# Choosing 256 tokens each of experts 0 and 1 during the last attention unit, and running their matmuls in the gaps of selection

## The chip, the cores and the metric

The kernel runs on one core of one Trainium2 chip. The metric is device time in microseconds (us); lower is better. Several executions are timed. Most of one kernel agree within about 1%; the kernel before has also slower ones (282 to 286 us, mean granted TensorE clock 0.94 to 0.956, against 277 to 280 us at 0.976 to 0.992). An execution over 1.5% above the fastest of its kernel is called slow, and only fast ones are compared here.

## The reference, cut to what matters

```python
x = attention(q, k, v)               # 4 batches x 768 tokens, 8 heads of 64: x is 3072 x 512
logits = x @ w_gate                  # 3072 x 8
order = argsort(-logits.flatten())   # greedy: best (token, expert) pairs first
for idx in order:                    # a token goes to its best expert that has room,
    tok, e = idx // 8, idx % 8       # each expert takes exactly 384 tokens
    if assigned[tok] < 0 and counts[e] < 384:
        assigned[tok] = e; counts[e] += 1
for e in range(8):
    out[assigned == e] = relu(x[assigned == e] @ w1[e]) @ w2[e]   # 512 -> 1024 -> 512
```

No expert knows all its tokens until the whole assignment is known. A few tokens can be known sooner: a token of the first three batches whose logit is high enough for its expert stays there whatever the fourth batch brings.

## The kernel before

Four stages follow one another: attention (eight units; each ends with sums that give its part of the logits), selection (four "rounds", a chain of small VectorE, TensorE and ScalarE steps), dispatch (the chosen tokens become row numbers, the "ids"), and experts. A round, with its useless matmuls that keep TensorE busy:

```python
pk = ps_d.tile([128, 2, 128], FP32, tag="pk")     # a PSUM tile of its own
# ... matmuls into pk ...
pn = ps_d.tile([128, 1], FP32, tag="pn")          # another PSUM tile
# ... matmuls into pn ...
fill(2)                                           # useless matmuls
nc.scalar.activation(Xe[:, nk : nk + 1], pn, AF.Identity, scale=-1.0, bias=bias232)
nc.vector.max(out=mx8, in_=pk)                    # reads pk, while ScalarE reads pn
# ... Xe, ranks; fill(1); next round ...
```

Experts. Each takes three slabs of 128 rows. The rows come by gathers (indirect transfers, one per slab), and the weights of experts 2 to 7 by twelve transfers of 1 MB ("tiles", two per expert). GpSimd issues all of them, and the scatters of the results too, in program order. Four tiles are issued before selection starts; the others here:

```python
gather(0); load_x(0); gather(1)                   # three slabs each
for e in range(8):
    late_weights()                                # one weight tile
    if e + 2 < 8: gather(e + 2)
    late_weights()                                # another
    # up: 32 matmuls of 384 columns, ReLU on ScalarE
    if e + 1 < 8: load_x(e + 1)                   # transposes of the next rows
    # down: 24 matmuls of 512 columns; scatter of each slab
```

`load_x(e + 1)` stands between up and down of expert e. If its rows are not there, the down matmuls wait behind it (6.0 us in the result below).

The softmax here doesn't subtract the row's maximum and nothing guards it: scores larger than these inputs give would overflow.

Of the kernel before, what the change touches and what calls it, by code (L numbers as in the profile page):

```python
# [38 lines left out]
W_EARLY = 2  # L39


@with_exitstack
def kernel(
# [75 lines left out]
    idn = consts.tile([128, NCHUNK], FP32)  # L119

# [8 lines left out]
    @later  # L129
    def _():  # L130
        nc.gpsimd.memset(negones, -1.0)
        nc.gpsimd.memset(bias232, float((32 * 128 - CAP) // 16))

# [40 lines left out]
    @later  # L174
    def _():
        nc.gpsimd.memset(eofs_bf, -63.5)
        iota(eofs_bf[0:1, :, :], [[0, NCHUNK], [CAP, N_EXP]])

# [7 lines left out]
    @later  # L186
    def _():
        for g_ in range(4):
            iota(idn[32 * g_ : 32 * g_ + 32, :], [[S_, B_], [32, NBLK]], base=192 * g_ - N_TOK // 2, cm=1)
        nc.gpsimd.tensor_copy(out=idc[:, ROT:NCHUNK], in_=idn[:, 0 : NCHUNK - ROT])  # L190
        nc.gpsimd.tensor_copy(out=idc[:, 0:ROT], in_=idn[:, NCHUNK - ROT : NCHUNK])

    @later
    def _():
        nc.gpsimd.memset(nb[:, 0:64], 1.0)
        nc.gpsimd.memset(Ub[:, 0:8, :], 0.0)
        nc.gpsimd.memset(Lb[:, 0:8, :], 0.0)

# [24 lines left out]
    QB = 384  # L223

    pctx = ExitStack()
    tp = pctx.enter_context(tc.tile_pool(name="tp", bufs=6, side="right"))
# [3 lines left out]
    with ExitStack() as actx:  # L230
# [4 lines left out]
        rawp = actx.enter_context(tc.tile_pool(name="rawp", bufs=1, side="right"))  # L235
        ttp = actx.enter_context(tc.tile_pool(name="ttp", bufs=4, side="right"))
# [249 lines left out]

        def warm(n):
            for _ in range(n):
                pw = ps_t.tile([128, 512], FP32, tag="pt", name="pw")
                nc.tensor.matmul(pw, lhsT=ones_bf, rhs=ones_bf[:, 0:1].to_broadcast([128, 512]), start=True, stop=True)  # L490
# [6 lines left out]
        if True:  # L497
# [98 lines left out]
            for u in range(2, NU + 1):  # L596
# [57 lines left out]
                for _ in range(3):  # L654
                    if late:
                        late.pop(0)()
                if wpieces:
                    weight_pieces(1 if u < 6 else 2, Bp)
            while late:
                late.pop(0)()  # L660

    w2pool = ctx.enter_context(tc.tile_pool(name="w2pool", bufs=1, reuse_waits="tile"))
    w1_late = [w2pool.tile([128, NKC, F_DIM], BF16, name=f"w1_{e}") for e in range(W_EARLY, N_EXP)]
    w2_late = [w2pool.tile([128, NFC, DM], BF16, name=f"w2_{e}") for e in range(W_EARLY, N_EXP)]
    lates = []
    for e in range(W_EARLY, N_EXP):
        lates.append((w1_late[e - W_EARLY], moe_w1[e].rearrange("(kc p) f -> p kc f", p=128)))
        lates.append((w2_late[e - W_EARLY], moe_w2[e].rearrange("(fc p) d -> p fc d", p=128)))
# [11 lines left out]
    def w1_of(e):  # L680
        return w1_early[:, e, :, :] if e < W_EARLY else w1_late[e - W_EARLY]

    def w2_of(e):
        return w2_early[:, e, :, :] if e < W_EARLY else w2_late[e - W_EARLY]

    idi = consts.tile([128, NCHUNK], I32)
    fi = consts.tile([1, 1], I32)

    def routing(general):
      with ExitStack() as dctx:  # L690
# [28 lines left out]
        def fill(n):  # L719
            for _ in range(n):  # L720
                pw = ps_d.tile([128, 512], FP32, tag="fill", name="pw")
                nc.tensor.matmul(pw, lhsT=ident_bf, rhs=w1_early[:, 0, 0, 0:512], start=True, stop=True)  # L722
# [19 lines left out]
        def fast_round(k, X, Dg):  # L742
            nk = 16 * k
            UB = best(X, Dg)
            pk = ps_d.tile([128, 2, 128], FP32, tag="pk", name="pk")
            for hf in range(2):
# [3 lines left out]
                                    in0=UB[:, 8:32, :], in1=bc_e(mn), op=ALU.is_gt)  # L750
            for hf in range(2):
                nc.tensor.matmul(pk[:, hf, :], lhsT=nb[:, 128 * hf : 128 * hf + 128], rhs=neg_bf,
                                 start=False, stop=True, skip_group_check=True)
            pn = ps_d.tile([128, 1], FP32, tag="pn", name="pn")
            for hf in range(2):
                nc.tensor.matmul(pn, lhsT=nb[:, 128 * hf : 128 * hf + 128], rhs=ones_bf[:, 0:1],
                                 start=(hf == 0), stop=(hf == 1))
            if X is None:
                tok_begin()
            fill(2)  # L760
            Xe = ditp.tile([128, 129], FP32, tag="Xe", name="Xe")
            nc.scalar.activation(Xe[:, nk : nk + 1], pn, AF.Identity, scale=-1.0, bias=bias232)
            mx8 = ditp.tile([128, 8], FP32, tag="mx8", name="mx8")
            nc.vector.max(out=mx8, in_=pk.rearrange("p a b -> p (a b)"))
# [8 lines left out]
            pr2 = ps_d.tile([128, 129], FP32, tag="pr2", name="pr2")  # L773
            nc.tensor.matmul(pr2[:, 0:nk], lhsT=Gm, rhs=Xe[:, 0:nk], start=True, stop=True)
# [4 lines left out]
            rk = ps_d.tile([128, 128], FP32, tag="rk", name="rk")  # L779
            for k0 in range(0, k, 4):  # L780
# [5 lines left out]
                for kk in range(k0, k0 + 4):  # L786
                    nc.tensor.matmul(rk[:, 0:nk], lhsT=Gm_bf, rhs=tg[:, kk, 0:nk],
                                     start=(kk == 0), stop=(kk == k - 1))
            tok_begin()
            fill(1)  # L790
# [22 lines left out]
        def dispatch():  # L813
            pR = ps_d.tile([128, CE], FP32, tag="X", name="pR")
            pc = ps_d.tile([96, 2], FP32, tag="pn", name="pc")
# [4 lines left out]
            nc.tensor.matmul(pR, lhsT=ones_bf[0:2, :], rhs=eofs_bf.rearrange("p c e -> p (c e)"),  # L820
# [10 lines left out]
            MAGIC = 1.5 * 2.0 ** 23  # L831
            hm = ditp.tile([128, NCHUNK], FP32, tag="hm", name="hm")
            nc.vector.tensor_scalar(out=hm, in0=dest, scalar1=1.0 / 128.0, scalar2=MAGIC, op0=ALU.mult, op1=ALU.add)
            hi = ditp.tile([128, NCHUNK], FP16, tag="hi", name="hi")
            nc.vector.tensor_scalar(out=hi, in0=hm, scalar1=-MAGIC, scalar2=None, op0=ALU.add)
            lo = ditp.tile([128, NCHUNK], FP16, tag="lo", name="lo")
            nc.vector.scalar_tensor_tensor(out=lo, in0=hi, scalar=-128.0, in1=dest, op0=ALU.mult, op1=ALU.add)
            fill(9)
# [7 lines left out]
            pI = ps_d.tile([128, NCHUNK], FP32, tag="rk", name="pI")  # L846
# [8 lines left out]
            fill(12)  # L855
# [4 lines left out]
        def general_path():  # L860
# [54 lines left out]
            def count(dst, m):  # L915
                pc = ps_d.tile([128, CE], FP32, tag="X", name="pc")
# [16 lines left out]
            with tc.For_i(0, N_EXP):  # L933
# [21 lines left out]
                pg = ps_d.tile([128, CE], FP32, tag="pk", name="pg")  # L955
# [18 lines left out]
        if True:  # L974
            X, Dg = None, None
# [3 lines left out]
            fill(2)  # L979
            nc.vector.tensor_tensor(out=M, in0=Ub[:, 8:32, :], in1=bc_e(mn), op=ALU.is_le)  # L980
            dispatch()
            pf = ps_d.tile([1, CE], FP32, tag="pr2", name="pf")
            nc.tensor.matmul(pf, lhsT=ones_bf[:, 0:1], rhs=Mf, start=True, stop=True)
            fc8 = dap.tile([1, N_EXP], FP32)
            nc.vector.tensor_reduce(out=fc8, in_=pf.rearrange("p (c e) -> p e c", e=N_EXP), axis=AX.X, op=ALU.add)
            fm = dap.tile([1, 1], FP32)
            nc.vector.tensor_reduce(out=fm, in_=fc8, axis=AX.X, op=ALU.max)
            nc.vector.tensor_single_scalar(out=fi, in_=fm, scalar=capf, op=ALU.is_gt)

    def experts(first):  # L990
        with ExitStack() as fctx:
# [3 lines left out]
            scatters = []  # L995
            xT_of = {}
            xes = {}

            def gather(e):
                for t in range(TSLAB):  # L1000
                    s = TSLAB * e + t
                    xe = gp.tile([128, DM], BF16, tag="xe", name=f"xe_{s}")
                    tc.keep_in_program_order(nc.gpsimd.indirect_dma_start(  # L1003
                        out=xe, out_offset=None, in_=x_tok[:, :],
                        in_offset=bass.IndirectOffsetOnAxis(ap=idi[:, s : s + 1], axis=0),
                    ))
                    xes[s] = xe

            def load_x(e):
                xT_e = fp.tile([128, NKC, TSLAB, 128], BF16, tag="xT_e", name=f"xT_{e}")  # L1010
                for t in range(TSLAB):
# [4 lines left out]
                    nc.vector.tensor_copy(out=xT_e[:, :, t, :], in_=pxe)  # L1016
                xT_of[e] = xT_e

            gather(0)
            load_x(0)  # L1020
            gather(1)
            for e in range(N_EXP):
                xT_e = xT_of.pop(e)
                if first:
                    late_weights()
                if e + 2 < N_EXP:
                    gather(e + 2)
# [3 lines left out]
                for fc in range(NFC):  # L1031
                    ph = ps_h.tile([128, CAP], FP32, tag="ph")
                    for kc in range(NKC):
                        nc.tensor.matmul(ph, lhsT=w1_of(e)[:, kc, 128 * fc : 128 * fc + 128],  # L1034
                                         rhs=xT_e[:, kc, :, :].rearrange("p t n -> p (t n)"),
                                         start=(kc == 0), stop=(kc == NKC - 1))
                    nc.scalar.activation(hT[:, fc, :], ph, AF.Relu)  # L1037
                if e + 1 < N_EXP:
                    load_x(e + 1)
                for t in range(TSLAB):  # L1040
                    po = ps_o.tile([128, DM], FP32, tag="po")
                    for fc in range(NFC):
                        nc.tensor.matmul(po, lhsT=hT[:, fc, 128 * t : 128 * t + 128],  # L1043
# [3 lines left out]
                    s = nc.gpsimd.indirect_dma_start(  # L1047
                        out=out[:, :],
                        out_offset=bass.IndirectOffsetOnAxis(ap=idi[:, TSLAB * e + t : TSLAB * e + t + 1], axis=0),
                        in_=ot, in_offset=None,  # L1050
                    )
                    for prev in scatters:
                        tc.declare_no_dep(s.ins, prev.ins, reason="each token has one expert: the rows written differ")
                    scatters.append(s)
# [4 lines left out]
    gp = ctx.enter_context(tc.tile_pool(name="gp", bufs=9, side="right", reuse_waits="tile"))  # L1059
    fp = ctx.enter_context(tc.tile_pool(name="fp", bufs=2, side="right", reuse_waits="tile"))  # L1060
    hp = ctx.enter_context(tc.tile_pool(name="hp", bufs=2, side="right", reuse_waits="tile"))
    op = ctx.enter_context(tc.tile_pool(name="op", bufs=4, side="right", reuse_waits="tile"))
    experts(True)
    flag = nc.values_load(fi[0:1, 0:1], engines=mybir.ALL_ENGINES)  # L1064
# [38 lines left out]
```

## Time and profile before

282.65 us median of 3 runs (277.18, 282.65 and 496.86; the last is an outlier, and 282.65 is a slow run by the rule above, so the fast state is at 277); the profiled run took 277.43. Stages, read from the starts and ends of the matmuls in the trace:

| event, us from the start | before |
|---|---|
| last attention unit starts | 116.4 |
| its last sums end | 139.4 |
| first selection matmul | 141.3 |
| dispatch starts | 163.9 |
| ids ready | 170.0 |
| first expert matmul | 177.3 |
| expert 2 starts | 199.2 |
| TensorE's last matmul ends | 266.1 |

The same stages as windows (start and end; length; busy time of the matmuls, weight loads, VectorE, ScalarE and GpSimd, with counts; granted clock; DMA share, which counts packets by their start and so can pass 1; GB/s), last unit to the end of TensorE's work:

```profile
116.40:139.40 23.00, 23.00 (x481) 19.67 (x480) 12.14 (x22) 8.73 (x14) 5.37 (x9) 1.00 0.61 109
139.40:141.30 1.90, 0.07 (x3) 0.06 (x1) 1.43 (x6) 0.00 (x0) 1.12 (x2) 1.00 1.05 167
141.30:163.90 22.60, 18.62 (x122) 11.22 (x122) 18.51 (x67) 1.95 (x8) 0.00 (x0) 1.00 1.12 196
163.90:170.00 6.10, 5.57 (x41) 2.65 (x42) 4.46 (x14) 0.00 (x0) 0.00 (x0) 1.00 0.24 49
170.00:177.30 7.30, 5.33 (x28) 1.96 (x27) 1.82 (x6) 0.00 (x0) 5.51 (x6) 1.00 0.29 80
177.30:199.20 21.90, 21.77 (x134) 12.11 (x134) 5.82 (x11) 7.84 (x16) 14.26 (x16) 1.00 1.02 203
199.20:266.10 66.90, 65.81 (x391) 36.05 (x395) 18.24 (x33) 23.52 (x48) 33.01 (x35) 1.00 0.73 185
```

Attention and the experts (rows 1, 6, 7) keep TensorE busy nearly all the time. In selection (row 3) its 18.6 us include useless matmuls.

GpSimd's issues in expert 2 (start, length, engine, line, operation, destination<-source, count, and in brackets the idle time before and what ended it):

```profile
201.38 0.82 POOL L673 DMA_DIRECT2D w<-in_moe_w_dram  x1
202.50 1.00 POOL L1003 DMA_INDIRECT xe<-x_tok,idi  x1 [0.30 <-issue]
...
207.20 0.94 POOL L673 DMA_DIRECT2D w<-in_moe_w_dram  x1 [1.20 <-DMA w<-in_moe_w_dram]
...
214.48 0.81 POOL L673 DMA_DIRECT2D w<-in_moe_w_dram  x1 [2.04 <-DMA w<-in_moe_w_dram]
215.60 0.99 POOL L1003 DMA_INDIRECT xe<-x_tok,idi  x1 [0.31 <-issue]
```

A gather (xe) is issued behind a weight tile (w), and GpSimd sometimes waits until an earlier tile has landed (1.20 and 2.04 us here). With experts of 11.1 us this just keeps up.

### The profile page before, as it was taken

What the parts mean: (1) busy time and instruction counts of PE and PEld (TensorE: products, weight loads), DVE (VectorE), ACT (ScalarE), POOL (GpSimd) and SP (SyncE); (2) the same over time, 40 slices, a digit from 0 to 9 for tenths busy, and PEclk for the clock granted to TensorE, in tenths of its full rate; (3) what the DMA queues carried; (4) which work ended last, traced back from release to release, by engine and by line L of the source; (5) the groups of instructions that cost most, each with busy time, mean ns of one, the idle gap of its engine ahead of it and who ended that gap; (6) DMA issues with size and microseconds to landing.
All of it is one profiled execution on the core that took longest, in us unless ns stands there. A gap on an engine that the chain in (4) does not pass through costs nothing. (4 is left out here: it accounts for less than half of the span.)

```text
span 275.6 us, 7465 instructions
## 1 busy us (share of the span) xinstructions
PE 250.6 (91%) x3174; PEld 172.7 (63%) x3182; DVE 160.0 (58%) x311; ACT 136.3 (49%) x224; POOL 82.6 (30%) x131
## 2 busy tenths in 40 slices
PE   7699899999999999999967878799999999999960
PEld 2577688888888888888844533355565545555520
DVE  3978998888969787774468875322423213233130
ACT  5998969596895959736200000144152250532500
POOL 5040000030508030110330002757665555741240
PEclk9999999999999999999999999999999999999996
DMA  7993889499799978282699990399999999430221
GB/s 275 330 266 66 218 196 275 86 222 261 121 318 160 251 148 182 66 152 62 103 195 206 194 181 13 108 183 187 267 258 263 263 245 290 165 133 10 107 89 36
DMA packets 52568, 49.27 MB, mean 179 GB/s; under 512 B 29744, under 2 KB 44080, under 8 KB 52528
## 3 DMA queue, kind: packets, MB, share of 16 engines
q0 software_dynamic: 15680, 26.22, 45.8%
q1 hardware_dynamic: 36848, 22.50, 31.3%
q8 instruction: 27, 0.44, 0.7%
q14 instruction: 13, 0.11, 0.1%
HBM read 56.05 MB, written 9.44 MB: 238 GB/s over the span
## 5 line engine op out<-in xcount | busy, mean ns | idle before, releaser
L1037 ACT ACTIVATE hT<-ph 128x384 bf16<-128x384 f32 x64 | 31.4, 490 | 69.3 <-PE ph L1034 68.6
L357 ACT ACTIVATE P<-ps 128x860 f32<-128x860 f32 (+1 forms) x46 | 39.4, 895 | 23.2 <-PE ps L339 22.5
L339 PE MATMUL ps<-qT,kA 32*128 32x215 f32 (+2 forms) x864 | 43.6, 333 | 2.5 <-ACT qT L304 2.5
L339 PEld LDWEIGHTS ps<-qT,kA 32*128 32x128 f32 x864 | 37.1, 185 | 7.2 <-ACT qT L304 3.0
L392 PE MATMUL po<-P,v 128*64 128x215 f32 (+6 forms) x576 | 40.6, 292 | 0.2 <-DVE P L372 0.2
L392 PEld LDWEIGHTS po<-P,v 128*64 128x64 f32 x576 | 34.4, 136 | 8.3 <-issue 3.1
L372 DVE TENSOR_TENSOR P<-P,Wm 128x860 f32<-128x860 f32 (+1 forms) x32 | 33.1, 1051 | 9.2 <-ACT P L357 6.5
L1003 POOL DMA_INDIRECT xe<-x_tok,idi x24 | 23.2, 968 | 37.9 <-PE pw L722 29.8
L1046 DVE COPY ot<-po 128x512 f32<-128x512 f32 x24 | 16.4, 691 | 30.2 <-PE po L1043 24.2
L1047 POOL DMA_INDIRECT out_dram<-ot,idi x24 | 23.6, 985 | 30.0 <-DVE ot L1046 27.0
L1034 PE MATMUL ph<-xT,w 128*128 128x384 bf16 x192 | 32.2, 326 | 0.0
L1043 PE MATMUL po<-w,hT 128*128 128x512 bf16 x138 | 31.7, 379 | 0.1
L1043 PEld LDWEIGHTS <-hT 128*128 128x128 bf16 x192 | 18.3, 98 | 19.5
L1016 DVE COPY xT<-pxe 128x512 bf16<-128x512 bf16 x24 | 9.5, 422 | 35.2 <-PE pxe L1015 34.2
L423 PE MATMUL pr<-P,onesx 128*32 128x168 f32 (+11 forms) x768 | 27.6, 259 | 0.0
L1034 PEld LDWEIGHTS <-w 128*128 128x128 bf16 x192 | 18.8, 98 | 13.1
L423 PEld LDWEIGHTS pr<-P,onesx 128*32 128x32 f32 x768 | 24.7, 109 | 2.3 <-issue 0.3
L289 ACT COPY kA<-tT_k 128x720 f32<-128x720 f32 (+2 forms) x18 | 24.4, 1358 | 0.2
L365 DVE TENSOR_TENSOR P<-P,Wm 128x860 f32<-128x860 f32 x16 | 16.3, 1050 | 8.8 <-ACT P L357 8.8
L397 ACT COPY oT<-po 128x384 f32<-128x384 f32 x32 | 14.9, 494 | 8.2 <-PE po L392 8.2
L468 PE MATMUL pk<-ident,oT 128*128 128x128 f32 x96 | 16.5, 288 | 2.2 <-DVE LT L439 2.0
L304 ACT COPY qT<-tT_q 128x768 f32<-128x768 f32 (+1 forms) x11 | 16.5, 1499 | 0.2 <-DVE tT_q L279 0.2
(151 smaller groups left out, 273.0 us busy)
## 6 DMA issues: line engine op xcount, KB each, us to landing
w<-in_moe_w_dram POOLq DMA_DIRECT2D x12, 1024.0 KB, 12.7
v<-in_v_dram SPq DMA_DIRECT2D x32, 180.0 KB, 2.8
kr<-in_k_dram SPq DMA_DIRECT2D x7, 768.0 KB, 4.5
qr<-in_q_dram SPq DMA_DIRECT2D x7, 768.0 KB, 7.6
w_early<-in_moe_w_dram POOLq DMA_DIRECT2D x8, 512.0 KB, 6.6
x_tok<-x SPq DMA_DIRECT2D x32, 96.0 KB, 3.2
w_early<-in_k_dram SPq DMA_DIRECT2D x1, 768.0 KB
w_early<-in_q_dram SPq DMA_DIRECT2D x1, 768.0 KB
```

The source lines that it names most:

```text
L289: nc.scalar.copy(out=kA[:, i0:i1, 8:128].rearrange("p i (c j) -> p i c j", j=NJ), in_=t[:, i0 * NC5 : i1 * NC5, :].rearrange("p (i c) j -> ...
L304: copy(out=qTs[u][:, g, NJ * c0 : NJ * c1].rearrange("p (c j) -> p c j", j=NJ), in_=tTs[f"q{u}", g].rearrange("p j c -> p c j")[:, c0:c1, :])
L339: nc.tensor.matmul(heads[a][:, o : o + w], lhsT=kA[r, gd, i, :], rhs=qTt[r, gd, KT * i : KT * i + w], start=(gd == 0), stop=(gd == 1), ski ...
L357: nc.scalar.activation(P[:, :, 0 : GW[g]], ps[w_][:, :, 0 : GW[g]], AF.Exp, scale=0.125)
L372: tt(out=P[:, :, 0 : GW[g]], in0=P[:, :, 0 : GW[g]], in1=Wm[:, h0 : h0 + 2, lo : lo + GW[g]], op=ALU.mult)
L392: nc.tensor.matmul(po[n][bk][64 * t : 64 * t + 64, a - QB * bk : z - QB * bk], lhsT=v7[:, t, i, :], rhs=P[:, t, o + a - q0 : o + z - q0], ...
L423: nc.tensor.matmul(o_, lhsT=l_, rhs=r_, start=first[gq], stop=True, skip_group_check=True)
L1003: tc.keep_in_program_order(nc.gpsimd.indirect_dma_start(out=xe, out_offset=None, in_=x_tok[:, :], in_offset=bass.IndirectOffsetOnAxis(ap=i ...
L1034: nc.tensor.matmul(ph, lhsT=w1_of(e)[:, kc, 128 * fc : 128 * fc + 128], rhs=xT_e[:, kc, :, :].rearrange("p t n -> p (t n)"), start=(kc == ...
L1037: nc.scalar.activation(hT[:, fc, :], ph, AF.Relu)
L1043: nc.tensor.matmul(po, lhsT=hT[:, fc, 128 * t : 128 * t + 128], rhs=w2_of(e)[:, fc, :], start=(fc == 0), stop=(fc == NFC - 1))
L1047: s = nc.gpsimd.indirect_dma_start(out=out[:, :], out_offset=bass.IndirectOffsetOnAxis(ap=idi[:, TSLAB * e + t : TSLAB * e + t + 1], axis= ...
```

## The change

In the last attention unit the kernel now chooses 256 tokens for each of experts 0 and 1, out of the first three batches, that are certain to stay there, gathers their rows, and lets their transposes and matmuls replace the useless ones in selection and dispatch. The last stage then has one slab for experts 0 and 1 instead of three. To make room for it in PSUM, some tiles of a round were put together. The diff, cut to its core:

```diff
+            e1_min(); ...; e1_pe(); ...; e8_pe()     # early choosing, between the steps of the last unit
+            e8_ids()                                  # early ids; four gathers, one per early slab
 ... cut ...
+        items = [] if general else early_work(ps_d)   # 4 row transposes, 64 up and 32 down matmuls
+        def work(us):                                 # takes items until their cost is used up,
+            ...                                       # useless matmuls when there are none left
 ... cut: in a round ...
-            pk = ps_d.tile([128, 2, 128], FP32, tag="pk", name="pk")
+            pkn = ps_d.tile([128, 512], FP32, tag="pk", name="pkn")
+            pk = pkn[:, 0:256].rearrange("p (a b) -> p a b", a=2)
+            if X is not None:
+                work(0.34)
-            pn = ps_d.tile([128, 1], FP32, tag="pn", name="pn")
+            pn = pkn[:, 256:257]
-            fill(2)
+            work(0.85 if X is not None else 0.6)
-            fill(1)
+            work(0.7)
 ... cut: in dispatch and behind it ...
-            fill(9)
+            work(3.2)
-            fill(12)
+            gather(0, range(ET, TSLAB), False)        # ET = 2: one slab is left
+            gather(1, range(ET, TSLAB), False)
+            gather(2, range(TSLAB), False)
+            while items:
+                work(0.1)
 ... cut: experts ...
+            def slabs(e):
+                return range(ET if first and e < 2 else 0, TSLAB)
                 if first:
                     late_weights()
-                if e + 2 < N_EXP:
-                    gather(e + 2)
+                if e + 2 < N_EXP and not (first and e == 0):
+                    gather(e + 2, slabs(e + 2))
                 if first:
                     late_weights()
```

## The prediction

> **What bounds it now.** TensorE, except in selection (busy time by stretches). Attention's last sums end near 139.4 us. Selection and dispatch (141.2 to 170) are a chain of small VectorE, TensorE and ScalarE steps, 5.2 us a round, whose TensorE gaps hold useless fills. From the first gather (170.3) to the first expert matmul (177.3) are 7 us, also filled. Then 88.8 us of experts, TensorE busy 87.6: 11.1 us each (5.2 up, 0.75 transposes, 5.2 down). Tail 9.5 us.
>
> **Removed (estimates from these durations).** In the last stage experts 0 and 1 have one slab of 128 tokens instead of three. Down loses 32 matmuls of about 0.215 us (6.9 us); up shrinks from 5.2 to about 2 us, twice (6 us); 16 transposes go (1 us): about 14 of 88.8 us. The first expert waits for one gather instead of three: 2.3 us more.
>
> **Added ahead of the experts.**
> - Early selection inside the last attention unit: TensorE 3.4 us (eight rank matmuls 0.5, eighteen id matmuls of 53 ns 0.95, fp32 steps the rest), VectorE 8.5 us, mostly in its idle time. Attention ends about 4.3 us later.
> - Transposes of early rows stand ahead of selection in TensorE's order, their gathers behind two weight pieces: 0.5 to 1.5 us.
> - Early items overrun the fills they replace slightly, and ReLU delays small ScalarE copies: 0.5 to 1 us.
> - In dispatch the down matmuls share one PSUM tile, so each group of eight waits for a ScalarE copy (0.7 to 0.9 us, from 0.49 us for 384 columns); the id matmuls come 1.3 us late.
> Ids come about 7 us later (5.5 to 8.5).
>
> **Where the expert gain goes.** GpSimd's DMA queue works in order: gathers issued at 202.5 and 215.6 landed at 214.6 and 227.4, each 0.4 us after the weight tile issued before them. A weight tile occupies it for 5 us alone, 6 to 7 us among gathers and scatters (landings of consecutive tiles). [...] The changed program issues three weight tiles (two of expert 4, one of 5) just ahead of expert 3's gathers, because experts 0 and 1 now take only 4 us each. I put the first tile 9.4 us after the ids; those gathers then land 28 to 31 us after the ids, while TensorE wants the rows in the middle of expert 2, 19 us after: a stall of 9 to 12 us (down of expert 2 stands behind it in program order), and 0 to 3 us more at experts 4 and 5. From ids to TensorE's end: 96.1 us before, 90 to 95 after.
>
> **Sum.** +7 - 3.5: 277.4 becomes about 280.5 us in the fast state. Without the stall about 270.
>
> **What shows it.** Ids at 177 instead of 170; first remaining expert 5 us after them; TensorE idle some 10 us in the middle of expert 2, released by the DMA into xe, weight tiles landing just before; GpSimd's weight issues waiting on earlier DMAs; experts 6 and 7 back to back at 11 us.
>
> **What would make it wrong.** Gathers overtaking weights, or weight tiles landing in under 5 us: 268 to 272. Early gathers landing late, or more PSUM waits in selection: 284 to 288.
>
> Chances: faster 0.17, within 2% 0.55, slower 0.28. Range 270.5 to 286.5.

## More of the kernel before

From the page of the kernel before: busy tenths in 40 slices of the span, the granted TensorE clock in tenths, and the busy share of the DMA engines.

```profile
PE   7699899999999999999967878799999999999960
PEclk9999999999999999999999999999999999999996
DMA  7993889499799978282699990399999999430221
```

TensorE (PE) is the busy engine, and its granted clock is 1.00 up to the end of its work at 266.1 us.

## The result

The changed kernel takes 288.08 us median (287.06 to 288.64, 4 runs); the kernel before, in the same job, 280.26 (277.18 to 496.86, 4 runs). The ratio is 1.0376, 95% interval 1.0322 to 1.0431: slower. A ratio here is the mean time of one kernel's fast runs over that of the other's, so it is not quite the ratio of the medians; the fast runs of the kernel before were two (277.18 and 277.88), so the loss is 10.4 us. The outputs are correct. The time lies above the range that was predicted.

From the page of the changed kernel, the same three rows:

```profile
PE   7799899999999999899969888848919999999960
PEclk9999999999999999999977999997986999999995
DMA  7992979399996994460589993249999999630221
```

There are two dips: in slices 21 and 22 (the clock is at half from 147.4 to 154.3 us), and in slices 27 to 31 (186 to 222 us), where TensorE is partly idle (busy 25.4 of 36.0 us) and the clock is at half again, from 195.2 to 198.6 and from 212.3 to 219.1 us. In the kernel before neither is there (clock 1.00 up to 271.0 us).

The same stages as windows:

```profile
116.70:146.60 29.90, 27.73 (x526) 23.04 (x525) 18.92 (x53) 9.42 (x16) 7.50 (x12) 1.00 0.51 98
146.60:149.30 2.70, 1.09 (x9) 0.77 (x8) 1.29 (x5) 1.07 (x2) 2.70 (x5) 0.65 0.58 87
149.30:175.80 26.50, 24.17 (x182) 18.64 (x182) 18.85 (x68) 7.61 (x18) 0.91 (x2) 0.91 1.03 178
175.80:183.20 7.40, 6.03 (x49) 3.37 (x50) 4.50 (x15) 1.17 (x2) 2.16 (x3) 1.00 0.30 81
183.20:188.90 5.70, 3.83 (x24) 1.61 (x23) 1.67 (x10) 1.17 (x2) 3.85 (x4) 1.00 0.34 104
188.90:202.30 13.40, 10.04 (x95) 6.81 (x93) 2.30 (x5) 3.95 (x16) 7.91 (x11) 0.87 0.81 158
202.30:277.00 74.70, 68.69 (x397) 37.09 (x395) 18.30 (x33) 23.59 (x48) 35.41 (x37) 0.95 0.78 185
```

Row by row against before: the unit is 6.9 us longer (29.9 against 23.0), the rows' transposes 0.8, the rounds 3.9 with the clock at 0.91, dispatch 1.3. With the unit's start 0.3 later, the ids come at 183.2 and not 170.0, which is 13.2 later. From there to the end of TensorE's work it is 93.8 us (277.0 - 183.2) against 96.1. Experts 0 and 1 are 8.5 us shorter (row 6), and the last row, which is the same work as before, 7.8 us longer.

TensorE in the timeline, lines with idle time before them (start, length, line, operation, operands, count, and in brackets the idle time and what ended it; "issue" means that the profile shows nothing that it waited for):

```profile
144.64 0.32 PE L468 MATMUL pr<-P,onesx 128*32 128x48 f32 x6 [0.26 <-issue]
145.37 0.53 PE L471 MATMUL pr<-oT,wgx 128*32 128x192 f32 x5 [0.41 <-issue]
...
147.51 0.91 PE L989 MATMUL px<-ident_bf,xeE 128*128 128x128 bf16 x7 [0.73 <-issue]
...
191.32 0.38 PE L1395 MATMUL ph<-xT,w_early 128*128 128x128 bf16 x4 [1.27 <-ACT hT L1398]
...
213.68 1.03 PE L1373 MATMUL pxe<-ident_bf,xe 128*128 128x128 bf16 x8 [6.01 <-DMA xe<-x_tok,idi]
```

The same transposes in the kernel before, with no wait ahead of them:

```profile
204.43 0.61 PE L1015 MATMUL pxe<-ident_bf,xe 128*128 128x128 bf16 x8
```

The last line of the changed kernel is the predicted stall: in the middle of expert 2 TensorE waits 6.0 us for the rows of expert 3. The first lines were not predicted: TensorE pauses at the end of attention, and the profile shows nothing that it waits for. I call this starvation below. The line at 191.32 is of the same kind, one engine on: in expert 0 the ReLUs on ScalarE come one in about 1.44 us though their inputs are ready, and TensorE waits for them.

What GpSimd issues around the stall:

```profile
192.60 1.78 POOL L941 DMA_DIRECT2D w<-in_moe_w_dram  x2
...
199.69 0.78 POOL L941 DMA_DIRECT2D w<-in_moe_w_dram  x1
200.78 1.03 POOL L964 DMA_INDIRECT xe<-x_tok,idi  x1 [0.30 <-issue]
202.11 0.99 POOL L964 DMA_INDIRECT xe<-x_tok,idi  x1 [0.30 <-issue]
203.41 0.94 POOL L964 DMA_INDIRECT xe<-x_tok,idi  x1 [0.30 <-issue]
```

Three tiles are issued between the ids and the gathers of expert 3 (200.78 on), and those rows are there at 213.7, 30.5 us after the ids.

One more pair of lines, the maximum on VectorE in a middle round. In the timeline of the kernel before:

```profile
148.61 0.43 DVE L764 MAX8 mx<-pk 128x8 f32<-128x256 f32 x1 [0.38 <-PE pn L756]
```

In that of the changed kernel:

```profile
158.45 0.43 DVE L1113 MAX8 mx<-pkn 128x8 f32<-128x256 f32 x1 [0.83 <-ACT Xe L1110]
```

In the kernel before, the maximum was released by TensorE, after 0.38 us of idle time; now it is released by ScalarE, which reads the neighbouring column of the same PSUM tile, after 0.83 us. Nothing in the arithmetic asks for that, and what puts the maximum behind ScalarE is not in the trace; what is there is 0.45 us more idle time.

### The profile page after: what moved, and what is told of

Its sections match the earlier page's. It is cut to its first block, busy times and chain, and to the rows that moved or that the text cites. A ratio compares the mean times of both kernels' runs of the same rounds, so it can differ in the third digit from the quotient of the medians.

```text
span 286.3 us, 7694 instructions
## 1 busy us (share of the span) xinstructions
PE 251.6 (88%) x3256; PEld 180.3 (63%) x3256; DVE 164.1 (57%) x342; ACT 142.2 (50%) x242; POOL 88.2 (31%) x151
## 5 line engine op out<-in xcount | busy, mean ns | idle before, releaser
L1398 ACT ACTIVATE hT<-ph 128x384 bf16<-128x384 f32 (+1 forms) x64 | 27.5, 438 | 57.1 <-PE ph L1395 53.6
L1404 PE MATMUL po<-w,hT 128*128 128x512 bf16 x144 | 35.0, 396 | 0.0
L1407 DVE COPY ot<-po 128x512 f32<-128x512 f32 x20 | 13.8, 691 | 32.7 <-PE po L1404 30.7
L1374 DVE COPY xT<-pxe 128x512 bf16<-128x512 bf16 x20 | 8.0, 423 | 38.3 <-PE pxe L1373 35.4
L972 POOL DMA_INDIRECT out_dram<-ot,idi x20 | 19.8, 992 | 31.0 <-DVE ot L1407 28.1
L1404 PEld LDWEIGHTS <-hT 128*128 128x128 bf16 x160 | 15.9, 103 | 17.5 <-issue 3.1
L964 POOL DMA_INDIRECT xe<-x_tok,idi x20 | 19.4, 969 | 12.8 <-DMA xe<-x_tok,idi 6.1
L442 ACT COPY oT<-po 128x384 f32<-128x384 f32 x32 | 14.8, 492 | 10.9 <-PE po L437 10.3
```

The source lines that it names most:

```text
L964: ins = nc.gpsimd.indirect_dma_start(out=xe, out_offset=None, in_=x_tok[:, :], in_offset=bass.IndirectOffsetOnAxis(ap=idi[:, s : s + 1], a ...
L972: s = nc.gpsimd.indirect_dma_start(out=out[:, :], out_offset=bass.IndirectOffsetOnAxis(ap=ids, axis=0), in_=ot, in_offset=None)
L1398: nc.scalar.activation(hT[:, fc, 0 : 128 * ns], ph[:, 0 : 128 * ns], AF.Relu)
L1404: nc.tensor.matmul(po, lhsT=hT[:, fc, 128 * j : 128 * j + 128], rhs=w2_of(e)[:, fc, :], start=(fc == 0), stop=(fc == NFC - 1))
```

## The experiments

Eighteen kernels ran in five jobs, each job on another chip: fifteen edits of the changed kernel, that kernel once more as a control, and two of the edited ones a second time. Times are medians, ratios are to the kernel before in the same job, whose median is given at the head of each job. "Stall" is the longest wait of TensorE for gathered rows in the experts. Two gave a wrong output.

### First job (before 282.48 median, its fast runs near 278.1)

**The gathers ahead of the weights.**

```diff
+                if first and e + 3 < N_EXP:
+                    gather(e + 3, slabs(e + 3))
                 if first:
                     late_weights()
-                if e + 2 < N_EXP and not (first and e == 0):
+                    late_weights()
+                elif e + 2 < N_EXP:
                     gather(e + 2, slabs(e + 2))
-                if first:
-                    late_weights()
```

> Edit: expert e+3's gathers are issued before the two weight tiles of round e, instead of e+2's between them; nothing else. Theory A (the gathers of expert 3 stand behind three weight tiles in one queue): TensorE's idle stretch of 6 us in the middle of expert 2 goes, and with it the half clock after it (7.3 us at 0.5, worth 3.6 us): 288 becomes about 279, ids still at 183. Rival B (the DMA engines are simply short of bandwidth there, or the stall is a wait of TensorE for something else): the idle moves to weights or scatters of experts 3 to 5 and the time falls by less than 3 us.

Measured: 288.29 us, ratio 1.0379, correct. (The half clock that the expectation puts at 7.3 us lasts 6.8 us in the trace of the result, and is worth 3.4.) The wait in expert 2 is gone, and another stands in expert 4:

```profile
237.76 0.59 PE L1373 MATMUL pxe<-ident_bf,xe 128*128 128x128 bf16 x4 [4.28 <-DVE xT L1374]
```

At that time GpSimd, which issues everything, had itself waited 5.6 us (to 236.6) for a scatter to land before it could issue the next tile. So the order alone is not the trouble, and the second theory holds: the weight traffic comes late as a whole, and whatever is behind it waits.

**The last two early weight pieces after the last sums.**

```diff
-            weight_pieces(2, 13)
 ...
             sums_out(15, pr)
+            weight_pieces(2, 15)
```

> Edit: the last two early weight pieces (1 MB read each) are issued after the last sums instead of in the middle of the last unit. Theory C (the TensorE gaps without a cause in the profile between 144.1 and 147.5 come from the traffic of these pieces and the early gathers, and the clock drop of 147.3 to 154.9 follows from those gaps): last sums take 2.0 us again instead of 4.0, the early rows land at once, the clock stays at 1.0, ids come 4 to 6 us earlier, time about 283. Rival D (the clock drops because the early selection's small matmuls keep the array too idle, whatever the DMA does): clock still 0.5 near 147 to 155, time 287 to 288.

Measured: 287.55 us, ratio 1.0346, correct. The pauses at the end of attention are the same (0.27, 0.44, 0.20 and 0.70 us): the pieces in front of the early gathers do not make them.

**Early choosing kept but not used** (fills and three slabs as before).

```diff
-        items = [] if general else early_work(ps_d)
+        items = []
 ... cut: no early gathers, full capacity and three slabs for experts 0 and 1 again
```

> Edit: early selection in the last attention unit stays as it is, but its choice is not used: no early gathers, no early expert work, fills as before, all experts with three slabs. It measures the cost of the early selection alone. Expected by the sum of its own matmuls and waits (3.6 + 1.3 us): 277.4 + 5 = 282 to 283, clock 1.0. If the selection's matmuls themselves bring the clock down (Rival D): 286 to 288 with the clock at 0.5 after unit 7.

Measured: 290.21 us, ratio 1.0432. The unit takes 28.1 us, 5.1 more than before, and has no pauses at its end: there are no early gathers in it. The granted clock is 1.00 from 117.4 to 145.5 us, and the four matmuls that open the first round take 0.71 us, against 1.22 at half clock in the result; so the choosing's small matmuls did not bring it down. The later stages of this run say nothing, because my useless matmuls, sized in steps of 0.22 us, came to about 2.2 us a round where the kernel before has three (0.65 us).

**Early work without choosing** (ids 0 to 511 fixed, results thrown away; wrong).

```diff
-            e1_min() ... e8_pe()              # all steps of the choosing
+        nc.gpsimd.iota(idiE, pattern=[[128, 2 * ET]], base=0, channel_multiplier=1)
```

> Edit: the early selection is taken out and the early ids are the constants 0 to 511; early gathers, early expert work in the gaps and one-slab experts 0 and 1 stay; early results go to a scratch tensor, so the output is wrong on purpose for the rows in slots 0 to 255 of experts 0 and 1. It measures what the moved work gives without what choosing costs. Expected if the late losses are those of the last stage (queue order): unit 7 as before, ids 2 to 4 us later than before, from ids to the end 93 us as in the change: 276 to 280. If the half clock and the gaps near 144 to 155 come with the early rows' transposes and not with the choosing, ids stay 6 us late or more: 283 and up.

Measured: 281.65 us, ratio 1.0134. The ids come at 176.8, 6.8 us later than before and not 2 to 4, without any choosing. The rounds are 2.9 us longer than before although no clock is lost in them (the four matmuls that open the first round take 0.68 us), so the clock is not the main cause; what is left is the early work and the PSUM placements, which this run keeps. The pauses moved with the gathers, from 144 to 147.5 us to 137.4 to 138.3, where they are shorter (0.16 and 0.24 us). The stall is 4.4 us.

### Second job (before 277.88 median)

**Early rows by plain transfers** (rows 0 to 511; wrong).

```diff
-                nc.gpsimd.indirect_dma_start(out=xe, ..., in_offset=...idiE...)
+                nc.sync.dma_start(xe, x_tok[128 * s : 128 * s + 128, :])
```

> Wrong result on purpose: the early rows are tokens 0 to 511, loaded by four plain transfers issued by SyncE instead of four gathers issued by GpSimd at 141.9 to 146.7; the early choosing and the early scatters stay. Theory (the run of gathers on GpSimd starves TensorE at 144.1 to 147.5, and the idle time takes the clock away in the first round): last sums take 2.0 us and not 3.8, attention ends near 144.5 instead of 146.6, the clock stays full from there to the dispatch (lost time below 0.5 us against 3.4), so the ids come 4 to 6 us earlier than in the changed kernel (183.2) and the time falls by 4 to 6 us, to 282 to 284. Rival (the gaps come with the place in the program, or with the weight tiles that follow): same gaps, same clock loss, time within 1 us of the changed kernel.

Measured: 283.29 us, ratio 1.0181. No pauses above 0.2 us, attention ends at 144.6, no clock is lost before the experts (the four matmuls that open the first round take 0.71 us), the ids come at 179.3. As the theory had it, in this job. TensorE still pauses in expert 0 (1.72 and 1.58 us): the gathers after the ids are still in place.

**Six tiles before the routing, none in expert 0, two each in experts 1 to 3.**

```diff
-    for _ in range(4):
+    for _ in range(6):
         late_weights(False)
 ...
-                if first:
-                    late_weights()
                 if e + 2 < N_EXP and not (first and e == 0):
                     gather(e + 2, slabs(e + 2))
-                if first:
+                if first and e > 0:
+                    late_weights()
                     late_weights()
```

> Six late weight tiles are issued ahead of the routing instead of four (the DMA engines are under 60% busy from 173 to 194 in the changed kernel), and in the experts the gather for e+2 goes ahead of the two weight tiles. Theory (the 6.0 us of idle TensorE in expert 2 is weight traffic that came too late, with the clock loss of 3.4 us behind it): no wait above 1 us on gathered rows in any expert, no clock loss in the experts, last stage (start of expert 2 to the end) 66 to 68 us instead of 74.7, time 279 to 282; the gathers at 184 may land up to 3 us later. Rival (GpSimd, which issues everything in order, is the limit, so the wait moves elsewhere as it did when the gathers were moved alone): a new wait of 3 us or more in another expert, time 286 to 289.

Measured: 288.47 us, ratio 1.0358, correct. The theory looked wrong: the wait in expert 2 is gone, but waits of 1.9 and 1.2 us follow in experts 4 and 5, and the ids are no earlier. Between 195 and 200 us the DMA engines moved nothing (0 GB/s, share 0.00): with no tile in expert 0 I had made a hole in the traffic and two tiles at once behind it.

**The early gathers in two pairs, a weight tile between them.**

```diff
+            egather(range(0, ET))             # in place of all four
 ...
     late_weights(False)
+    egather(range(ET, 2 * ET))
     for _ in range(3): late_weights(False)
```

> The early gathers in two pairs with the issue of one weight tile between them. If a run of three or more gathers in a row is what starves TensorE: gaps at the end of attention under half of the changed kernel's (idle below 1 us between 143 and 148), time 2 to 4 us lower. If any gather does it, or if the gathers are not the cause: the gaps stay or move with the second pair, time within 1 us of the changed kernel.

Measured: 284.46 us, ratio 1.0211, correct: about 4 us under the two other correct kernels of this job, which have other edits (no control ran here). One pause of 0.31 us is left at the end of attention, and no clock is lost in the rounds (0.71 us for the four matmuls that open the first).

**Less early work in the rounds and in dispatch.**

```diff
-                work(0.34)
+                work(0.0)
-            work(0.85 if X is not None else 0.6)
+            work(0.6)
-            work(0.7)
+            work(0.6)
-            work(3.2)
+            work(1.5)
```

> Less early work placed inside the rounds (0.6 us per round and not 1.9) and in the dispatch (1.5 us and not 3.2); what is left runs after the ids, where TensorE waits for rows. Theory (the work placed in the chain is longer than the gaps): rounds 1.5 to 2.5 us shorter, dispatch 1.0 to 1.5 us shorter, ids 2.5 to 4 us earlier (179 to 181); given back in part as the leftover then delays the first expert by 1.5 to 3 us; time 286 to 288. Rival (the rounds' overrun is the slow clock and the starvation alone): ids within 1 us of 183.2, time 288 to 291.

The edit leaves 1.2 us a round (twice 0.6), not the 0.6 of the expectation. Measured: 288.42 us, ratio 1.0353. The rounds take 25.3 us and the dispatch 6.0 (26.5 and 7.4 in the result). The ids come 2.6 us earlier (180.6) and nothing is won: the work that is left over pushes the early scatters, and behind them the weight tiles, back, and the stall is 6.6 us.

### Third job (before 281.54 median, its fast runs 277.0 to 279.8)

**Six tiles before the routing, and one per expert behind its gathers.**

```diff
-    for _ in range(4):
+    for _ in range(6):
         late_weights(False)
 ...
-                if first:
-                    late_weights()
                 if e + 2 < N_EXP and not (first and e == 0):
                     gather(e + 2, slabs(e + 2))
                 if first:
                     late_weights()
```

> Six weight tiles ahead of the routing, and then one tile for each of the first six experts, issued behind the gather for e+2 (the run before had none in the first expert and two in the next three, and stayed at 288.5 with short waits of 1.9 and 1.2 us in experts 4 and 5). Theory (the 6.0 us wait in expert 2 is weight traffic ahead of the gather in the queue): no wait on gathered rows above 1 us in any expert, clock lost in the experts below 0.5 us, last stage 67 to 69 us against 74.7, time 279.5 to 283. Rival (GpSimd or the DMA engines as a whole are the limit): waits of 3 us or more in sum appear in later experts, time 286 or more.

Measured: 274.01 us, ratio 0.9843 (0.9777 to 0.9909), correct. That is 14 us under the changed kernel's first runs, in another job, below the 279.5 to 283 expected, and 1 to 2% under the kernel before. There is no stall; the window from the start of expert 2 to the end shows TensorE busy all the time at full clock:

```profile
197.90:263.80 65.90, 65.90 (x397) 36.09 (x395) 18.37 (x33) 23.52 (x48) 34.99 (x37) 1.00 0.84 189
```

Its issues after the ids, one tile ahead of the gathers of expert 3 and not three:

```profile
192.57 0.83 POOL L941 DMA_DIRECT2D w<-in_moe_w_dram  x1
...
196.03 0.99 POOL L964 DMA_INDIRECT xe<-x_tok,idi  x1 [0.30 <-issue]
```

The two tiles more go where the engines were idle: in the dispatch the DMA share is 1.17 and behind the ids 0.77, against 0.30 and 0.34. But the profile had no pauses at 144 to 147.5 either, though the program is the same there as in the run with six tiles of the job before. That made the starvation suspect.

**Two PSUM placements.**

```diff
-            pn = pkn[:, 256:257]
+            prk = ps_d.tile([128, 512], FP32, tag="pr2", name="prk")
+            pn = prk[:, 256:257]
 ...                                           # early outputs alternate
+                    if (e + t) % 2: pos[e, t] = ps_f.tile([128, DM], FP32, tag="ph", bufs=2)
```

> Two PSUM placements of the changed kernel undone: the count column of a round is written to another bank than the values whose maximum VectorE takes (in the changed kernel both are in one tile, and the maximum starts 0.54 us after the count and waits on ScalarE's reading of it, against 0.17 us before), and the early outputs alternate between three banks instead of one. Theory (the sharing costs about 0.37 us in each of four rounds, and 0.67 us for each of two outputs that fall into the dispatch): rounds 1.2 to 1.6 us shorter, dispatch (counts to ids) 6.1 to 6.3 us against 7.4, ids 2.5 to 3 us earlier, time 284.5 to 286.5. Rival (the rounds' overrun is the early matmuls in front of the chain on TensorE): rounds within 0.5 us of 26.5, time 287 or more.

Measured: 284.22 us, ratio 1.0206, correct. (What the expectation calls a bank is where a PSUM tile lies; the traces show tiles, not banks.) The rounds take 24.8 us (26.0 in the run with six tiles of this job, 26.2 in the control below), the dispatch 6.0 (7.3 in both), the ids come at 179.6. The maximum is again released by TensorE:

```profile
156.60 0.43 DVE L1117 MAX8 mx<-pkn 128x8 f32<-128x256 f32 x1 [0.46 <-PE prk L1109]
```

The stall grew to 8.9 us: TensorE reached it at 201.4 us, against 207.7 in the result, and the rows came at 210.2, against 213.7.

**All repairs** (split gathers, six tiles, PSUM, and the transposes of expert 1's early rows moved ahead of their use).

```diff
+        items += [rows(0, 0), rows(0, 1)] + ups[0][0] + ups[0][1] + [rows(1, 0)] + ups[0][2] + [rows(1, 1)] + ups[0][3]
```

> All repairs at once: gathers split by a weight tile, six tiles early and one per expert, the two PSUM placements, and the transposes of the second expert's early rows moved one step ahead of their use. If the terms add (split -3.7, stall -6 to -8, banks -2.7, rows -1.0): 271 to 275, 2 to 3% under the kernel before. If they hide behind one another: 277 to 281, no better than before. The starvation in the first expert (3 to 4 us with its clock loss) is still there.

Measured: 272.82 us, ratio 0.9812 (0.9731 to 0.9893), correct: the lowest median of all, and within what was expected if the terms add. But the tiles alone had given 274.01, so the other repairs add 1.2 us and not 7; the intervals of the two ratios overlap. The ids come at 178.9, but the first gather is issued only at 182.5, after GpSimd has waited 3.7 us for a DMA; its rows land at 186.2, behind the sixth tile (183.8). TensorE waits 4.2 us for them, and the clock falls to half for 3.4 us (the 32 up matmuls behind the wait take 3.10 us, those of expert 1 at full clock 2.11). That the sixth tile is the cause is not shown: with five tiles such a wait comes back in the last run below.

**The same with GpSimd pausing between its issues after the ids.**

```diff
+            pause()                            # a memset of 128 x 400, three times
 ... cut: the gathers of expert 2 moved behind the early work, between the pauses
```

> The same, with GpSimd's run of five gathers and two scatters after the ids broken up by three memsets of about a microsecond. If a run of indirect transfers starves ScalarE in the first expert as it starved TensorE at the end of attention: the first expert's up matmuls take 2 to 3 us and not 5.8, no clock loss there, 2 to 4 us less than the run without pauses. If it is not the run: no difference above 1 us, or slower by the pauses.

Measured: 273.93 us, ratio 0.9851, correct. Inconclusive: in this job ScalarE was not starved in expert 0 in the run without pauses either. The kernel is about a microsecond slower. A memset took 0.45 us, half of what was meant.

### Fourth job (before 277.81 median): controls

**The changed kernel again, without an edit.**

> The changed kernel itself, unaltered, as a control. If the starvation belongs to the kernel: gaps without a shown cause at 144 to 147.5 again, last sums 3.8 us, time 287 to 289. If it belongs to the chip it ran on: on a chip without it, last sums near 3.5 us with waits on the early rows instead, first expert's up matmuls 2 to 3 us and not 5.8, and a time of 282 to 286.

Measured: 286.01 us, ratio 1.0307. TensorE's waits from the end of attention to the stall, the lines that answer to those of the first run:

```profile
146.16 0.40 PE L989 MATMUL px<-ident_bf,xeE 128*128 128x128 bf16 x4 [1.56 <-DMA xeE<-x_tok,idiE]
147.50 0.60 PE L989 MATMUL px<-ident_bf,xeE 128*128 128x128 bf16 x4 [0.95 <-DMA xeE<-x_tok,idiE]
...
211.44 1.03 PE L1373 MATMUL pxe<-ident_bf,xe 128*128 128x128 bf16 x8 [10.53 <-DMA xe<-x_tok,idi]
```

So the starvation does not belong to the kernel alone; the chip, the session or the way in which the run was traced takes part: here the last sums run without a pause (attention ends at 144.6), and the first up matmuls take 2.2 us instead of 5.8. And it explains little of the loss. TensorE arrives earlier at expert 2 and waits 10.5 us there instead of 6.0; the kernel is still 3% slower than before.

This trace has the landings of GpSimd's transfers too. Of the three tiles between the ids and the gathers of expert 3, the first and the third (issued at 190.8 and 193.9; KB, and us from issue to landing):

```profile
w<-in_moe_w_dram POOLq DMA_DIRECT2D x1, 1024.0 KB, 8.6
...
w<-in_moe_w_dram POOLq DMA_DIRECT2D x1, 1024.0 KB, 17.2
```

The third lands at 211.1, and TensorE's wait for the rows issued behind it ends at 211.4.

**Six tiles and one per expert, again; and the split gathers, again.** No edit.

> The kernel with six early tiles and one per expert, unaltered, with the control on the same chip. If its 274 us hold whatever the chip: 273 to 276, 12 to 14 us under the control. If part of it was the chip: it shows the starvation whenever the control does, and 276 to 281; the difference to the control is then 7 to 10 us.

> The kernel with the split gathers, unaltered, with the control on the same chip. If the run of gathers starves TensorE: 3 to 4 us under the control where the control is starved. Where the control is not starved: within 1.5 us of it.

Measured: 275.10 us, ratio 0.992 (0.987 to 0.997), for the tiles, 10.9 us under the control: it holds on another chip, and with no starvation to hide in. Against the kernel before it is within 2%. 285.65 us, ratio 1.029, for the split gathers: 0.4 us under the control. In the second job they had come out 4.0 us under kernels with other edits; here, without starvation, there was next to nothing to win.

**All repairs, five early tiles, and useless matmuls where TensorE waits.**

```diff
+            fill(9)                            # ahead of the early rows' transposes
+            fill(7)                            # ahead of the first expert
 ...
+                if first and e == 0:
+                    late_weights()             # the tile that was taken from the front
```

> All repairs with five early tiles (so that the first gathers after the ids do not queue behind the sixth) and matmuls without use where TensorE waits for the early rows (nine, 2 us) and for the first expert's rows (seven, 1.5 us), so that it is not idle there. Theory (the clock falls to half for 3.4 us after each of these waits, 1.7 us lost each): no loss before the end of the kernel, first rows 1 to 2 us sooner, time 267 to 270.5. Rival (the clock falls for another reason, or the fills delay the rows): 272 to 275 as in the run of all repairs.

Measured: 278.70 us, ratio 1.0026, correct: my mistake, and a good test. With two tiles ahead of expert 3's gathers the stall is back:

```profile
206.61 1.04 PE L1391 MATMUL pxe<-ident_bf,xe 128*128 128x128 bf16 x8 [7.36 <-DMA xe<-x_tok,idi]
```

Up to that wait the clock is full (1.00 from 144.7 to 172.0 us; the up matmuls of expert 0 take 2.15 us), and the rounds take 23.3 us, 0.7 more than before the change.

### Fifth job (before 278.67 median, its fast runs 276.6 to 278.7)

**One tile per expert again, five early tiles; with and without useless matmuls (seven and four).**

```diff
-                if first and e == 0:
-                    late_weights()
```

> All repairs, five early tiles, then one per expert behind its gathers, with seven and four matmuls without use (0.43 us each in the run before) where TensorE waits. Theory (the wait in expert 2 is the tiles queued ahead of expert 3's gathers): with one tile there, not two, no wait above 1 us in the experts where the run before had 7.4; no clock loss before the end; ids at 177 to 178.5, ids to the end of TensorE's work 81 to 84 us, time 267 to 270.5. Rival (five early tiles are too few, the queue is the limit): a wait of 3 us or more, 273 to 278.

> The same without the fills. If the clock falls because TensorE waits: half clock for 3.4 us after the early rows' wait and, if that wait is long enough, after the first gather's, 1.2 to 3.4 us lost, ids 1 to 1.5 us later, time 1 to 3 us over the run with fills. If the fills change nothing: within 0.7 us.

Measured, five rounds each: 277.06 us, ratio 0.9962, with them; 273.65 us, ratio 0.9852, without. Both miss the 267 to 270.5 expected: from the ids to the end of TensorE's work they take 88.2 and 89.8 us, not 81 to 84; experts 0 and 1 alone take 13.7 and 11.4 against 8.0 in the control. The stall is gone in both (the longest wait in expert 2 is 1.3 us), so one tile there is enough. The expectation about the useless matmuls was wrong in its first half: no clock is lost in the rounds of either run (1.00 in both), and without them selection starts 1.6 us earlier. Its second half came true in the profile: without them TensorE waits 5.5 us for the first gather, which is issued 5.9 us after the ids, and the clock is at half for 10.2 us (181.9 to 192.1). ScalarE's starvation in expert 0 is in this job again (up takes 6.4 us with useless matmuls). The two profiled runs have nearly the same span (274.1 and 274.5) although the medians differ by 3.4 us: the profile without useless matmuls is of that kernel's slowest run (276.26; the other five took 273.27 to 274.91), so its long wait need not be in the others. Why the kernel with them is slower stays open.

## Why the prediction was wrong

**The step that failed is "Ids come about 7 us later (5.5 to 8.5)".** They came 13.2 us later in the result and 11.4 later in the control. Everything behind the ids was sized right, so the error went nearly whole into the time. The prediction had named "more PSUM waits in selection" among what would make it wrong, at 284 to 288 us, and had not put them into the sum. The terms of the sum, as predicted and as measured (differences of the windows to the kernel before):

| term | predicted | result | control |
|---|---|---|---|
| last attention unit | 4.3 | 6.9 | 5.1 |
| transposes of the early rows | 0.5 to 1.5 | 0.8 | 1.4 |
| the rounds ("0.5 to 1 us") | 0.5 to 1 | 3.9 | 3.6 |
| dispatch | 1.3 | 1.3 | 1.2 |
| start of the unit | 0 | 0.3 | 0.1 |
| ids | 5.5 to 8.5 | 13.2 | 11.4 |

- *The rounds* are the mis-sized term. I had costed the early items by their own durations and overlooked two things. First, the change puts the count column and the values of the maximum into one PSUM tile, and the maximum then waits for ScalarE (0.83 us idle before it in a middle round, against 0.38); I read the diff's PSUM merging as harmless there, though I had seen the same effect in dispatch. Undoing the PSUM placements made the rounds 1.2 us shorter than in the run with six tiles of the same job, 1.4 shorter than in the control. Second, the clock: in the changed kernel it falls to half in the first round, after TensorE's short waits around the transposes (from 147.4 to 154.3 us in the result). Three runs have the same placements and a full clock there (early work without choosing, plain rows, split gathers in the second job): their rounds take 25.5 to 25.7 us, so the clock is worth 0.5 to 0.7 us of the control's 26.2. With both out of the way (all repairs with five early tiles, three runs) the rounds take 23.3 to 23.6, 0.7 to 1.0 above before, which is the size I had predicted for the early items alone. These parts make 2.4 to 3.1 of the 3.6 us, from different jobs; the rest, perhaps the place of the transposes, no run separates.
- *The clock.* In the result the granted clock was 0.50 for 6.83 us from 147.4, for 3.41 from 195.2 and for 6.83 from 212.3, with 40.96 and 13.65 us of full clock between them; each of these is a whole multiple (2, 1, 2, 12 and 4) of 3.41 us. In the control it was 0.50 for 3.4 us in the first round (mean 0.94 from 144.6 to 174.1 us), and for 10.2 around its stall of 10.5 (mean 0.94 from 195.5 to 274.5). In the first round it went down behind two waits for the early rows, 1.56 and 0.95 us. All seven traces with two such waits there, 2.5 to 3.0 us in sum (the four runs of the third job, and of the fourth the control, six tiles and split gathers), lost the clock at that place; one wait alone, 1.83 us in the kernel before, was followed by a clock of 1.00. No experiment varied the waits by themselves, so how long a wait takes the clock away is not shown. The prediction gave the clock no term. Of the 10.2 us only the 4.3 behind the stall (211.4 to 215.8) cost anything, about 2.2 us by my estimate.
- *The choosing* took 5.1 us and not 4.3: the run with the choosing alone and the control agree. The 1.8 us more in the result go with the starvation, which the control does not have.

**The mechanism behind the ids was right, and so was its size.** From ids to the end of TensorE's work I predicted 90 to 95 us; it took 93.8 (result) and 93.1 (control). The first tile was issued 9.4 us after the ids in both, as predicted. I predicted that the rows of expert 3 land 28 to 31 us after the ids, and a stall of 9 to 12 us; the rows came 30.5 and 30.0 us after the ids, and the stall was 6.0 in the result, where starvation had already used up part of it, and 10.5 in the control. Of the 0 to 3 us more at experts 4 and 5 neither run shows a wait above 0.7 us. Nine runs with the changed kernel's order of tiles and gathers show how fixed this is (ids; end of the wait in expert 2; difference):

| run | ids | wait ends | difference | stall |
|---|---|---|---|---|
| result | 183.2 | 213.7 | 30.5 | 6.0 |
| control | 181.4 | 211.4 | 30.0 | 10.5 |
| early pieces late | 183.9 | 214.2 | 30.3 | 4.9 |
| early work, no choosing | 176.8 | 206.5 | 29.7 | 4.4 |
| plain rows | 179.3 | 209.3 | 30.0 | 4.8 |
| split gathers | 179.9 | 210.5 | 30.6 | 5.7 |
| split gathers, again | 181.6 | 211.5 | 29.9 | 10.4 |
| PSUM placements | 179.6 | 210.2 | 30.6 | 8.9 |
| less work | 180.6 | 214.1 | 33.5 | 6.6 |

TensorE's speed in experts 0 and 1 does not enter (eight of the nine differences are 29.7 to 30.6 us, with stalls of 4.4 to 10.5): the chain runs from the ids through GpSimd's issues and the weight tiles to the rows of expert 3. So starvation there (4 us more or less) only moves time between "slow" and "waiting", and removing it there alone should win nothing; no run did only that. An earlier id does count, one to one, except where GpSimd is held up behind the ids ("less work", whose scatters came later). In the kernel before, the 54 tiles, gathers and scatters that GpSimd issues from 170.3 to 263.7 us land in the order of their issue (173.4 to 266.4). The others agree: in the control the three tiles land at 199.4, 205.4 and 211.1 us and the wait of 10.5 ends at 211.4; with two tiles ahead (all repairs with nine and seven useless matmuls) they land at 200.6 and 205.5 and the wait of 7.4 ends at 206.6; with one (six tiles, third job) it lands at 201.4 and there is no wait.

**Where the expert gain of 14 us went.** The work is gone: experts 0 and 1 together take 8.0 us in the control against 21.9. But the same twelve tiles must be moved in less time. The engines were near idle from 164 to 177 us in the kernel before, and they still are after the change (0.29 and 0.34 of their time between dispatch and the first expert), while the eight tiles that are left are issued from 190.8 us on (control). Two tiles moved into that hole, and one in front of each gather, gave 10.9 us back in the control's job. "Without the stall about 270" was 4 to 5 us too low for the same reason as the whole: the ids.

**What stays open.** Why an engine with its data at hand pauses (0.2 to 0.7 us on TensorE, ReLUs about 1.44 us apart on ScalarE) while GpSimd issues indirect transfers (one in about 1.3 us). In the jobs that have it, it went away without the early gathers, moved when they moved, and was smaller where they were split, so they take part in it; but two of five jobs did not have it with the same instructions. The traces differ in one more way: where the pauses are (result, first, second and fifth job) no landing of GpSimd's transfers is recorded, and where they are not (third and fourth job) 43 to 60 of its 68 are. So the tracing, and not the chip, may be what differs; no run tells. That instructions come late is another guess of mine that no experiment tests. Nothing in the trace names what was missing.

## What to carry to other kernels

Taking work off the busiest engine shortens the time in which everything else must arrive; before doing it, count what must still be moved in that time, and look for the hole earlier in the kernel into which it can go. Here a chain of small steps paid 1.2 to 1.4 us for merged PSUM tiles and 0.5 to 0.7 us for the half clock behind idle time of TensorE, so cost the two as terms of their own, not as slack. And before a pause without a shown cause is explained, run the unchanged kernel again on the chip of the experiment: here one control took the weight from a theory that several runs had seemed to support.
